# Fewer warming matmuls, a smaller first session, an earlier piece of w_out and re-placed sessions in a fused attention and feed-forward kernel

## The chip, the cores and the metric

One core of a Trainium2 chip. The metric is the device time of one execution in microseconds (us), the median of several runs. All profiled runs told here are of the state called fast (within 1.5% of the kernel's fastest). The span of a trace is some 2 us shorter than the time. Runs of one kernel scatter by about 1 us here (314.31 to 315.16 for the kernel before in the last series), with one at 316.2 in another series, so differences below that need many runs and are told with an interval. The series ran on different chips, with the kernel before timed beside the others each time; its median was 314.70 to 314.82 in all of them.

## The reference, cut to what matters

```python
# q, k, v: (8 batches, 8 heads, 576 positions, 64); w_in (512, 2048), w_out (2048, 512)
scores = scale * q @ k.T;  mask = |i - j| <= 32;  attn = softmax(scores where mask)
x = (attn @ v) with heads side by side              # 4608 tokens x 512
h = x @ w_in
g = h >= 1 ? h : h <= -1 ? 0 : (h + 1)**2 / 4
out = g @ w_out
```

Attention only looks 32 positions to each side, so nearly all of the work is the two products of the feed-forward part.

## The kernel before: the parts that matter

The feed-forward part goes in steps a = 0, 1, ... 151. Step a works on the token tile t = a // 8 (256 tokens) and the block f = a % 8 of 256 hidden units: eight matmuls ("hp", w_in times xT, the attention output laid out for them), then ScalarE ("rr") and VectorE ("mx", "gT") make g of it. The products with w_out ("op") follow some steps later; for the first two tiles they are cut into *pairs* of eight matmuls, and a pair's result (its accumulator) is added up over several steps. Matmuls write to PSUM, the memory behind TensorE; a *pool* hands out buffers of it, and who asks for a buffer waits until the last reader of its former content is done. All attention work is hung into these steps by `at(step, ...)`, where a half step such as 13.5 means behind the pairs of step 13: `tposes` transposes q or k of a batch on TensorE and copies it out of PSUM on ScalarE and VectorE, `scores` makes masked scores and their exponentials ("pt"), one call being a *session* (its first matmuls, "bias", lay the mask), `sums` multiplies with v and with ones and divides, which gives xT. Before step 0 stands the start: batch 0's first positions go through all of this with TensorE otherwise empty, and matmuls on zeros (`keep_warm`, "z") are meant to keep its clock up.

```python
ps_h = tile_pool("ps_h", bufs=2, PSUM)      # hp of most steps
ps_s, ps_n = ...                            # one tile of two banks each: transposes, scores, sums
ps_o = tile_pool("ps_o", bufs=2, PSUM)      # accumulators of op, made after the start
# ... cut ...
keep_warm(14, ps_h, "hp")
qn[0, 0] = cast(q32, "qb", 5)               # waits for the load of q
qq = [tpose(0, n, 0, ...) ...]; kk = [tpose(0, n, 1, ...) ...]
scores(0, (0, 1), (0, 2), (0, 2), None)
scores(0, (0, 2), (0, 1), (2, 3), None, ps_n)     # the small session
scores(0, (1, 2), (0, 2), (0, 2), None, ps_p)
keep_warm(5, ...); e0 = sums(0, 0, 0, 256); keep_warm(2, ...); e1 = sums(0, 1, 0, 256, ps_p)
keep_warm(8, ...); e0(); e1()
# ... cut ...
pairs = [(8, 0), (9, 1), (10, 2), (11, 3), (12, 4), (13, 5), ...]    # (step, pair)
two_on_act = (1, 2, 7, 8, 9, 10, 11, 12)          # steps that square on ScalarE
# ... cut: the main loop ...
for a in range(...):
    flush()                                       # multiplications that finish xT, on VectorE
    hp = (ps_o if a in (6, 7) else ps_h).tile(...)
    # eight matmuls into hp; rr on ScalarE; mx and gT on VectorE (or mx on ScalarE)
    flush(); run(a)                               # what at(a, ...) has put here
    for x in post: pair(x)                        # the pairs of this step
    run(a + 0.5)
```

## Time and profile before

| | before |
|---|---|
| median of its runs | 314.72 us |
| span of the profiled run | 313.0 us (its time 315.1) |
| TensorE idle from 15 to 30 us, from 30 to 70 us | 2.45 us, 1.70 us |

The prediction below shows the rows on which it rests. One place that it tells in words only is step 13, the first scores of batch 1. The rows are TensorE's timeline of the kernel before, with start, length, engine, source line, result and operands:

```profile
38.58 1.20 PE L187 MATMUL tp<-ident,kn 128*64 128x128 bf16 x36
39.71 1.05 PE L445 MATMUL op<-w_out,gT 128*128 128x256 bf16 x8
40.59 1.04 PE L489 MATMUL hp<-xT,w_in 128*128 128x256 bf16 x8
41.56 0.41 PE L206 MATMUL bb<-bias,ident 64*64 64x512 bf16 x4
41.80 0.66 PE L227 MATMUL bb<-qT,kT 64*64 64x128 bf16 x16
42.39 1.05 PE L445 MATMUL op<-w_out,gT 128*128 128x256 bf16 x8
43.58 0.41 PE L206 MATMUL bb<-bias,ident 64*64 64x512 bf16 x4
```

How to read it: matmuls are pipelined, so the length of a row (1.05) is longer than its pitch. Take starts instead: 39.71, 40.59, 41.56 are eight matmuls each, 0.87 apart, plus 0.1 when the kind changes. So up to 41.56 TensorE streams. The 16 score matmuls have 0.66 where others of the kind have 0.42: a short stop inside, for the second copy of kT. From the pair at 42.39 to the masks at 43.58 it is 1.19 instead of 0.97: a hole of 0.22 that the bracketed waits do not show, because the modelled end of the pair covers it.

### The profile page before, as it was taken

What the parts mean: (1) busy time and instruction counts of PE and PEld (TensorE: products, weight loads), DVE (VectorE), ACT (ScalarE), POOL (GpSimd) and SP (SyncE); (2) the same over time, 40 slices, a digit from 0 to 9 for tenths busy, and PEclk for the clock granted to TensorE, in tenths of its full rate; (3) what the DMA queues carried; (4) which work ended last, traced back from release to release, by engine and by line L of the source; (5) the groups of instructions that cost most, each with busy time, mean ns of one, the idle gap of its engine ahead of it and who ended that gap; (6) DMA issues with size and microseconds to landing.
All of it is one profiled execution on the core that took longest, in us unless ns stands there. A gap on an engine that the chain in (4) does not pass through costs nothing.

```text
span 313.0 us, 8615 instructions
## 1 busy us (share of the span) xinstructions
PE 304.1 (97%) x3711; PEld 207.9 (66%) x3711; DVE 243.7 (78%) x380; ACT 196.2 (63%) x324; POOL 72.3 (23%) x88
## 2 busy tenths in 40 slices
PE   8988999999999999999999999999999999999995
PEld 3566878776666666666666666666666666666652
DVE  3359558878888888888888888888888888878760
ACT  2788886866765766567666666566676666654431
POOL 8797354653051314040604000000000000000000
PEclk9999999999999999999999999999999999999999
DMA  9999999999999989896996792006501000100111
GB/s 151 183 186 198 175 207 186 179 160 163 165 176 139 111 175 159 74 110 133 166 109 69 76 154 69 34 36 112 109 36 36 37 34 36 37 36 34 48 55 67
DMA packets 124102, 34.54 MB, mean 110 GB/s; under 512 B 108192, under 2 KB 119712, under 8 KB 124064
## 3 DMA queue, kind: packets, MB, share of 16 engines
q0 software_dynamic: 94720, 18.06, 77.9%
q1 hardware_dynamic: 29200, 15.63, 21.4%
q8 instruction: 29, 0.48, 0.6%
q10 hardware_dynamic: 144, 0.29, 0.4%
q14 instruction: 9, 0.07, 0.1%
HBM read 36.70 MB, written 9.44 MB: 147 GB/s over the span
## 4 chain that ended last, share of the span: by engine, by line
PE 90%; ACT 4%; DVE 3%; issue 1%; ACTq 0%
PE hp L489 38%; PE op L429 36%; PE bb L293 6%; PE op L445 4%; PE bb L227 2%; PE z L336 2%; ACT pt L235 2%; PE tp L187 1%; DVE xT L305 1%; ACT rc L300 1%; ACT lr L299 1%; DVE kT L190 1%; DVE qT L190 1%; DVE mx L500 1%; ACT rr L493 0%
## 5 line engine op out<-in xcount | busy, mean ns | idle before, releaser
L489 PE MATMUL hp<-xT,w_in 128*128 128x256 bf16 x1152 | 149.3, 273 | 2.0 <-DVE xT L308 1.2
L493 ACT ACTIVATE rr<-hp 128x512 f32<-128x512 f32 x144 | 85.6, 595 | 87.1 <-PE hp L489 86.2
L489 PEld LDWEIGHTS <-w_in 128*128 128x128 bf16 x1152 | 112.0, 98 | 41.6 <-issue 2.6
L429 PE MATMUL op<-w_out,gT 128*128 128x512 bf16 x512 | 130.4, 380 | 0.0
L500 DVE TENSOR_TENSOR mx<-hp,rr 128x512 f32<-128x512 f32 x136 | 93.7, 689 | 33.2 <-ACT rr L493 31.3
L501 DVE SCALAR_TENSOR_TENSOR gT<-rr,mx 128x512 bf16<-128x512 f32 x136 | 94.1, 692 | 4.6
L429 PEld LDWEIGHTS <-gT 128*128 128x128 bf16 x512 | 47.5, 98 | 36.8
L235 ACT ACTIVATE pt<-bb 128x1024 bf16<-128x1024 f32 (+1 forms) x33 | 33.2, 1012 | 4.6 <-PE bb L227 3.1
L106 POOL DMA_DIRECT2D vn<-in_v_dram x32 | 27.3, 864 | 35.4 <-PE bb L227 32.3
L305 DVE TENSOR_TENSOR xT<-bb,rc 128x512 bf16<-128x512 f32 (+1 forms) x32 | 21.0, 657 | 11.0 <-ACT rc L300 10.3
L434 ACT COPY osb<-op 128x512 f32<-128x512 f32 x32 | 18.6, 583 | 11.6 <-PE op L429 11.1
L300 ACT ACTIVATE rc<-lr 128x512 f32<-128x512 f32 (+2 forms) x40 | 23.5, 587 | 1.3
L299 ACT ACTIVATE lr<-bb 128x512 f32<-128x512 f32 (+2 forms) x40 | 22.0, 550 | 0.8 <-PE bb L293 0.7
L98 POOL DMA_DIRECT2D qn<-in_q_dram x10 | 12.2, 1222 | 43.1 <-DMA qT<-qn 37.8
L293 PE MATMUL bb<-pt,ones 64*64 64x256 bf16 (+3 forms) x352 | 19.5, 255 | 1.5 <-DVE kT L190 0.8
L201 DVE TENSOR_TENSOR pt<-pt,mask 128x1024 bf16<-128x1024 bf16 (+1 forms) x33 | 20.2, 613 | 0.1
L293 PE MATMUL bb<-pt,vn 64*64 64x128 bf16 (+3 forms) x712 | 18.2, 204 | 0.0
L293 PEld LDWEIGHTS <-ones 64*64 64x64 bf16 x352 | 10.2, 105 | 9.9 <-issue 9.9
L293 PEld LDWEIGHTS <-vn 64*64 64x64 bf16 x712 | 16.7, 107 | 0.0
L445 PE MATMUL op<-w_out,gT 128*128 128x256 bf16 x128 | 16.5, 273 | 0.0
L98 POOL DMA_DIRECT2D kn<-in_k_dram x10 | 12.1, 1214 | 10.0 <-DMA kT<-kn 3.8
L227 PE MATMUL bb<-qT,kT 64*64 64x128 bf16 x520 | 13.2, 217 | 0.3 <-DVE kT L190 0.2
(56 smaller groups left out, 120.8 us busy)
## 6 DMA issues: line engine op xcount, KB each, us to landing
out_dram<-osb SPq DMA_DIRECT2D x36, 256.0 KB, 2.3
vn<-in_v_dram POOLq DMA_DIRECT2D x32, 144.0 KB, 8.9
qn<-in_q_dram POOLq DMA_DIRECT2D x10, 288.0 KB, 7.4
kn<-in_k_dram POOLq DMA_DIRECT2D x10, 288.0 KB, 8.0
w_out<-in_moe_w_out_dram POOLq DMA_DIRECT2D x4, 512.0 KB, 12.5
w_in<-in_moe_w_in_dram POOLq DMA_DIRECT2D x12, 128.0 KB, 6.4
qn<-in_q_dram POOLq DMA_DIRECT2D x2, 576.0 KB, 13.5
kn<-in_k_dram POOLq DMA_DIRECT2D x2, 576.0 KB, 14.7
```

Of the source, the lines that this page charges most:

```text
L98: nc.gpsimd.dma_start(out=x[:, :, h], in_=src[b, NY * h:NY * h + NY].rearrange("y s d -> (y s) d") .rearrange("(u p) d -> p u d", p=128))
L106: nc.gpsimd.dma_start(out=vn[b][64 * a:64 * a + 64, :, h], in_=v[b, y:y + 2].rearrange("y s d -> (y s) d") .rearrange("(c r) d -> r c d", ...
L235: A.activation(p, ps[:, :, :128 * n].rearrange(like, y=m), AF.Exp, scale=D ** -0.5)
L293: nc.tensor.matmul(bb[HD[h], a, o + c0:o + c1], ones[HD[a]] if c is None else vn[b][HD[a], c, h], p(a, h), start=n == 0, stop=True, skip_g ...
L299: A.activation(lr[:, :, :D0], bb[:, :, D0:2 * D0], AF.Ln)
L300: A.activation(rc[:, :, :D0], lr[:, :, :D0], AF.Exp, scale=-1.0)
L429: nc.tensor.matmul(o, gT[tt // 2][:, j, 128 * (tt % 2):128 * (tt % 2) + 128], w_out[:, j], start=not done, stop=len(done) == 2 * NF - 1, s ...
L445: nc.tensor.matmul(o[:, tt], gT[p][:, j, 128 * tt:128 * tt + 128], w_out[:, j, 256 * half:256 * half + 256], start=not done, stop=len(done ...
L489: nc.tensor.matmul(hp[:, j], w_in[:, kk, 256 * f + 128 * j:256 * f + 128 * j + 128], xT[:, kk, r0:r0 + TB], start=n == 0, stop=n == 3)
L493: A.activation(rr, hp, AF.Relu, scale=0.5, bias=0.5)
L500: V.tensor_max(mx, hp, rr)
L501: V.scalar_tensor_tensor(g, rr, 1.0, mx, op0=ALU.min, op1=ALU.mult)
```

## The change

It means to start earlier (fewer warming matmuls, less in the small session), to fill the wait of step 8 with pair 0 (whose piece of w_out is therefore cut out and loaded ahead of the last two pieces of w_in), to give two score sessions different buffers, to square step 2 on VectorE and not on ScalarE, and to put other work between batch 2's transposes and the next user of their buffers.

```diff
-        keep_warm(14, ps_h, "hp")
+        keep_warm(11, ps_h, "hp")
...
-        scores(0, (0, 2), (0, 1), (2, 3), None, ps_n)
+        scores(0, (0, 2), (0, 1), (2, 3), None, ps_n, 32)      # 32 queries instead of 128
...
-        keep_warm(5, ps_h, "hp")
+        keep_warm(4, ps_h, "hp")
...
-        keep_warm(8, ps_h, "hp")
+        keep_warm(7, ps_h, "hp")
...
-    put(w[:4] + [(load_half, ...) ...] + w[4:])
+    put(w[:4] + [(load_half, ...) ...] + w[4:12])
+    put([(load_w_out, 0, 0, 4)] + w[12:])
...
-    pairs = [(8, 0), (9, 1), (10, 2), (11, 3), (12, 4), (13, 5), ...]
-    two_on_act = (1, 2, 7, 8, 9, 10, 11, 12)
+    pairs = [(6, 0), (8, 1), (9, 2), (10, 3), (11, 4), (13, 5), ...]
+    two_on_act = (1, 7, 8, 9, 10, 11, 12)
...
     # seq[n]: (sums, scores) of batch 1 and up, in order
-    at(14, seq[0][0], (*seq[1][0], ps_s))
-    sums of seq[2..5] at 18, 20, 22, 27;  scores of seq[0..6] at 13, 13.5, 16, 18, 20, 25, 27
+    at(13, seq[0][1]); at(13.5, (*seq[1][1], ps_n)); at(14, (*seq[0][0], ps_s), seq[1][0])
+    sums of seq[2..5] at 18, 21, 24, 27;  scores of seq[2..6] at 16, 18, 21, 25, 27
-    transposes of batch 2 at 19.5, 21.5
+    transposes of batch 2 at 19.5, 22.5
```

(The scheduling lines at the end are written shorter than in the file.)

More of the change, by code (lines that the diff above doesn't have):

```diff
@@ L111, in load_w_in, with load_w_out @@
                             in_=moe_w_in.rearrange("(h y d) f -> h d y f", h=2, d=64)[h][:, :, c0:c1])
-    def load_w_out(c, n):
-        nc.gpsimd.dma_start(out=w_out[:, 8 * n:8 * n + 8, 256 * c:256 * c + 256],
-                            in_=moe_w_out.rearrange("(ko ki) f -> ki ko f", ki=128)[:, 8 * n:8 * n + 8,
-                                                                                    256 * c:256 * c + 256])
+    def load_w_out(c, k0, k1):
+        nc.gpsimd.dma_start(out=w_out[:, k0:k1, 256 * c:256 * c + 256],
+                            in_=moe_w_out.rearrange("(ko ki) f -> ki ko f", ki=128)[:, k0:k1, 256 * c:256 * c + 256])
     early = ctx.enter_context(tc.tile_pool(name="early", bufs=1))
@@ L149 @@
     w += [(load_w_in, c, c + 256, h) for c in range(1536, DFF, 256) for h in range(2)]
-    put(w[:4] + [(load_half, 1, t, h) for t in range(2) for h in range(2)] + w[4:])
+    put(w[:4] + [(load_half, 1, t, h) for t in range(2) for h in range(2)] + w[4:12])
+    put([(load_w_out, 0, 0, 4)] + w[12:])
     P.tensor_copy(band[HD[1], 0:128], band[HD[1], 64:192])
@@ L154 @@
                       band[:, :x].rearrange("p (n j) -> p n j", n=1).to_broadcast([128, n, x]))
-    put([(load_w_out, 0, n) for n in range(2)] + [(load_rows, 1, t) for t in range(2)])
-    put([(load_v, 1, n) for n in range(4)] + [(load_w_out, 1, n) for n in range(2)])
+    put([(load_w_out, 0, 4, 8), (load_w_out, 0, 8, 16)] + [(load_rows, 1, t) for t in range(2)])
+    put([(load_v, 1, n) for n in range(4)] + [(load_w_out, 1, 8 * n, 8 * n + 8) for n in range(2)])
     put([(load_rows, 2, t) for t in range(2)] + [(load_v, 2, n) for n in range(4)])
@@ L209, in add_mask, with scores @@
                                  start=True, stop=False, skip_group_check=True)
-    def scores(b, ys, pars, cs, eng, pool=ps_s):
+    def scores(b, ys, pars, cs, eng, pool=ps_s, w=128):
         if b not in pt:
@@ L218, in scores @@
             cols = (ys[1] - ys[0]) * (pars[1] - pars[0]) * (cs[1] - cs[0])
-            add_mask([ps[:, h] for h in range(2)], cols, 128)
+            add_mask([ps[:, h] for h in range(2)], cols, w)
         for y1 in range(*ys):
@@ L226, in scores @@
                             s0 = S * (y1 + 2 * a) + 64 * c
-                            nc.tensor.matmul(ps[HD[a], h, 128 * n:128 * n + 128], kT[b][HD[h], s0:s0 + 64],
-                                             qTs[b % 3][HD[h], PAD + s0 - 32:PAD + s0 + 96],
+                            nc.tensor.matmul(ps[HD[a], h, w * n:w * n + w], kT[b][HD[h], s0:s0 + 64],
+                                             qTs[b % 3][HD[h], PAD + s0 - 32:PAD + s0 - 32 + w],
                                              start=eng is not None, stop=True, skip_group_check=True)
                     n += 1
-        p = pt[b][:, :, ys[0]:ys[1], pars[0]:pars[1], 128 * cs[0]:128 * cs[1]]
+        p = pt[b][:, :, ys[0]:ys[1], pars[0]:pars[1], 128 * cs[0]:128 * cs[1] - 128 + w]
         m = 2 if n > cs[1] - cs[0] else 1
@@ L234, in scores @@
         like = "p h (y j) -> p h y j"
-        A.activation(p, ps[:, :, :128 * n].rearrange(like, y=m), AF.Exp, scale=D ** -0.5)
+        A.activation(p, ps[:, :, :w * n].rearrange(like, y=m), AF.Exp, scale=D ** -0.5)
         mask(eng, p, mask4[:, :256 * n].rearrange("p (h j) -> p h j", h=2).rearrange(like, y=m))
@@ L377 @@
     NF = DFF // 256
-    pairs = [(8, 0), (9, 1), (10, 2), (11, 3), (12, 4), (13, 5), (15, 6), (15, 8), (16, 7), (17, 9)]
-    two_on_act = (1, 2, 7, 8, 9, 10, 11, 12)
+    pairs = [(6, 0), (8, 1), (9, 2), (10, 3), (11, 4), (13, 5), (15, 6), (15, 8), (16, 7), (17, 9)]
+    two_on_act = (1, 7, 8, 9, 10, 11, 12)
     ev = {}
@@ L399 @@
     seq = [x for b in range(1, B) for x in steps(b, 224)]
-    at(14, seq[0][0], (*seq[1][0], ps_s))
-    for n, a in enumerate((18, 20, 22, 27)):
+    at(13, seq[0][1])
+    at(13.5, (*seq[1][1], ps_n))
+    at(14, (*seq[0][0], ps_s), seq[1][0])
+    at(16, seq[2][1])
+    for n, a in enumerate((18, 21, 24, 27)):
         at(a, seq[2 + n][0])
-    for n, a in enumerate((13, 13.5, 16, 18, 20, 25, 27)):
-        at(a, seq[n][1])
+    for n, a in enumerate((18, 21, 25, 27)):
+        at(a, seq[3 + n][1])
     sl = [30, 32, 35, 39, 42, 45, 49, 52, 56, 59, 62, 65, 69, 73, 77, 81, 84, 88, 92]
@@ L408 @@
         at(a, seq[6 + n][0], seq[7 + n][1] if n < len(sl) - 1 else None)
-    for b, *a in ((1, 11, 12), (2, 19.5, 21.5)):
+    for b, *a in ((1, 11, 12), (2, 19.5, 22.5)):
         for t in range(2):
```

## The prediction

> **What bounds the kernel now.** I read the page's busy table first, then the waits of TensorE in its timeline, then VectorE and ScalarE around each wait. In a timeline row the first number is the start, the second the length, both in us; the bracket is the idle time before it and what ended it.
>
> ```profile
> PE 304.1 (97%) x3711; PEld 207.9 (66%) x3711; DVE 243.7 (78%) x380; ACT 196.2 (63%) x324; POOL 72.3 (23%) x88
> ```
>
> TensorE is the bound; only its idle time and its useless work can be had. The table by stretches says where:
>
> ```profile
> 15.00:30.00 15.00, 12.55 (x243) 9.71 (x242) 10.80 (x18) 12.70 (x23) 12.71 (x18) 1.00 1.37 191
> 30.00:70.00 40.00, 38.30 (x614) 32.08 (x613) 28.91 (x44) 29.64 (x48) 19.89 (x21) 1.00 2.00 182
> 70.00:300.00 230.00, 230.00 (x2646) 154.95 (x2645) 196.22 (x298) 142.78 (x238) 27.40 (x28) 1.00 0.82 92
> ```
>
> From 70 us on TensorE is busy without a hole (230.00 of 230.00), so whatever it is ahead or behind at 70 us is carried to the end unchanged. The holes are 2.45 us before 30 us and 1.70 us from 30 to 70. TensorE's timeline names them:
>
> ```profile
> 1.19 6.11 PE L336 MATMUL z<-warm 128*128 128x512 bf16 x14 [1.19 <-DVE warm L127]
> 7.13 0.67 PE L189 MATMUL tp<-ident,qb 128*128 128x128 bf16 x9
> ...
> 18.75 1.03 PE L489 MATMUL hp<-xT,w_in 128*128 128x256 bf16 x8 [0.37 <-DMA w_in<-in_moe_w_in_dram]
> ...
> 23.42 1.03 PE L489 MATMUL hp<-xT,w_in 128*128 128x256 bf16 x8 [0.23 <-DMA w_in<-in_moe_w_in_dram]
> ...
> 29.40 1.03 PE L489 MATMUL hp<-xT,w_in 128*128 128x256 bf16 x8 [1.17 <-DVE xT L308]
> ...
> 59.98 0.30 PE L293 MATMUL bb<-pt,ones 64*64 64x256 bf16 x4 [0.76 <-DVE qT L190]
> ...
> 66.31 0.28 PE L293 MATMUL bb<-pt,ones 64*64 64x192 bf16 x4 [0.77 <-DVE kT L190]
> ```
>
> The matmuls of feed-forward step a ("hp", eight of 256 columns, pitch 0.87) stand at 18.75 for a=2, 23.42 for a=4, 29.40 for a=8. Two of these are anchored on w_in pieces that only the DMA stream can move; 29.40 is anchored on VectorE, which from 25.07 works in one unbroken row:
>
> ```profile
> 25.07 0.62 DVE L305 TENSOR_TENSOR xT<-bb,rc 128x448 bf16<-128x448 f32 x1 [0.55 <-ACT rc L300]
> 25.61 0.68 DVE L500 TENSOR_TENSOR mx<-hp,rr 128x512 f32<-128x512 f32 x1
> 26.33 0.69 DVE L501 SCALAR_TENSOR_TENSOR gT<-rr,mx 128x512 bf16<-128x512 f32 x1
> 26.94 0.62 DVE L305 TENSOR_TENSOR xT<-bb,rc 128x448 bf16<-128x448 f32 x1
> 27.47 0.68 DVE L500 TENSOR_TENSOR mx<-hp,rr 128x512 f32<-128x512 f32 x1
> 28.19 0.69 DVE L501 SCALAR_TENSOR_TENSOR gT<-rr,mx 128x512 bf16<-128x512 f32 x1
> 28.80 0.55 DVE L308 TENSOR_TENSOR xT<-bb,rc 128x384 bf16<-128x384 f32 x1
> 29.27 0.68 DVE L500 TENSOR_TENSOR mx<-hp,rr 128x512 f32<-128x512 f32 x1
> ```
>
> **What the Trainium skill says.** "TensorE: Matmul & The Clock Gate", Part 1, gives the array half clock until about one busy window of 3.4 us, 426.7 ns per 512-column matmul cold and 215.7 warm. The trace agrees in size: 14 warming matmuls fill 1.19 to 7.13, 0.42 each, and the nine transposes after them take 0.67, that is warm; so the clock came up near 7.1, 5.9 us after the first matmul. Part 4 of the page says that transposes do not count as busy in the same way; no row of the kernel before tests that. Part 2 says that matmuls stay in program order and only weight loads are pulled ahead: a waiting matmul holds up all behind it, as the 1.17 at 29.40 did.
>
> **The change part by part.**
>
> *Warming and the small session.* The queries land and are cast by 5.84 (VectorE's cast row, 5.05 + 0.79). With 14 warming matmuls the transposes start at 7.13; with 11 the stream ends at 1.19 + 11 x 0.427 = 5.89. The nine q transposes then run cold, 0.107 each (estimate, a quarter of a 512-column cold matmul), to 6.85; the k half issued second at 1.95 lands 4.9 us later, at 6.85, so its transposes start near 7.0. VectorE's two copies (pitch 0.63) end about 8.5 instead of 9.19, and scores start some 0.8 earlier. The small session's exponential goes from 512 to 128 elements a partition: ScalarE's pitch over the three sessions is 0.92 for 1024 and 0.48 for 512, so 0.86 ns an element, 384 fewer is 0.33. The two warming matmuls of 0.216 taken out later only fit the shorter wait. Sum: the first xT is ready about 1.1 us earlier, step 1 ends about 16.1 instead of 17.2.
>
> *What becomes of these 1.1 us.* The second halves of k are issued last at 10.99 and land 6.3 later, 17.28; w_in for a=2 at 12.27 plus 6.4, 18.6; w_in for a=4 at 16.37 plus 6.9, 23.3. The stream in front of them is the same bytes in the same order. So hp of a=2 stays at 18.75 and hp of a=4 at 23.42: TensorE just waits longer, about 1.5 before 18.75 and 1.1 before 23.42. Of this part I expect 0 at the end, and nearly 0 as well if the clock came up later.
>
> *ScalarE and VectorE to step 8.* They do gain: the q and k copies end 1.1 earlier, and a=2 no longer squares on ScalarE (0.63). I put the multiplication at 25.07 at 24.45. But next comes mx of a=4, which needs rr of a=4, which needs hp of a=4, anchored: rr from 24.50 instead of 24.95, mx from 25.11 instead of 25.61. From there the row above repeats unbroken, 0.50 earlier: xT at 28.30 to 28.85, mx of a=6 at 28.77 to 29.45.
>
> *Pair 0 at a=6.* Its eight matmuls (0.87) move ahead of the wait of 1.17; w_out's piece of 256 KB lands at about 25.04 + 1.3 = 26.4 (512 KB took 2.6 between landings), and the last w_in at 27.7, in time. With xT at 28.9, a gain of 1.3 would seem due. But the pair takes a buffer of the two-buffer PSUM pool that hp of a=6 and a=7 use as well. Pair 0's accumulator holds one over several steps, so hp of a=7 must take that of a=6, and wait until mx of a=6 has read it: 29.45, start 29.50. Before, at 29.40 TensorE had done hp of a=7 and not pair 0; now, at 29.50, pair 0 and not hp of a=7. Equal work: 0.10 later. Expected gain of the move: none.
>
> *Pair 4 from a=12 to a=11.* Before, pair 4 and hp of a=13 filled the 1.75 between the k transposes (38.58 to 39.71) and the scores. Now only hp does. The copies hang on rr of a=12, which moves with hp of a=12: 37.61 before, now 38.57 (0.10 behind plus pair 4 ahead of it, 0.87). So the second copy of kT ends at 42.00 + 0.96 = 42.96, and TensorE stands about 1.0 before or inside the scores: 0.95 behind.
>
> *Session of 13.5 to the other pool.* Before, its masks waited for the exponential of the session at 13: the pair of a=13 at 42.39, masks at 43.58, about 0.30 of hole. That goes: 0.62 behind.
>
> *Batch 2 and its sums.* The sums at a=20 and 22 sat right behind the transposes and waited for their copies in the same pool: 0.76 and 0.77 in the rows, 0.92 and 0.93 if counted from the last matmul's stream instead of its modelled end (start to start 1.82, less 0.87). At a=21 and 24 there are another hp and an output group of 0.87 each between; the copies end some 1.8 after the transposes, so both holes close: -1.85.
>
> Sum at 70 us: +0.10 + 0.85 - 0.33 - 1.85 = -1.23. Time 314.74 - 1.23 = 313.5; I predict **313.4**, since I may have made the stall of a=13 a little too long.
>
> **The rivals.** (1) The step-7 buffer does not bind (the pool finds another, or the mx comes sooner). For it: the author moved pair 0 there to fill the 1.17. Then steps 7 and 8 run on at 28.1 and 29.0, 1.3 more is gained, and the time is about 312.1. Against it: two buffers, and the accumulator is live. (2) The start is worth what it looks like, 1.1 us to the end: 312.4. Against it, the two DMA waits that are there already in the kernel before. (3) The clock comes up a whole window later because transposes do not count: scores run cold, the first xT comes near 15.5 as before, and the slack before 18.75 and 23.42 swallows it: the time stays about 313.5. If the clock stayed low beyond 23 us it would cost microseconds, 316; I give that 2%. (4) The stalls of a=20 and 22 move rather than go, to the scores of batch 2 at a=25: 314.5 to 315. The copies will have been done for two steps, so I doubt it.
>
> **Range and chances.** Main line 313.5, rival 1 at 312.1, rival 4 at 314.5: 8 times in 10 between 312.0 and 314.2. Two per cent is 6.3 us, more than all holes after the start together (4.15 in the table), so faster 0.01, within 0.98, slower 0.01.
>
> **What would show each step.** hp of a=2 still near 18.75 and of a=4 near 23.42 with longer DMA waits: anchors right. hp of a=7 waiting for VectorE's mx (L500) until about 29.5: buffer right; hp of a=8 waiting for xT or nothing: wrong. Scores near 43 behind the kT copies with a hole of about 1: right. No wait on copies near 60 and 66: right. VectorE's q-copy at start near 7.1 instead of 7.84: clock and casts right. I would be wrong altogether if the w_in pieces land more than half a microsecond apart from before, as all steps to a=8 hang on them.

## The result, and the profile after

The changed kernel took 313.94 us, median of 4 runs, against 314.72 for the kernel before: ratio 0.9977, 95% interval 0.996 to 0.9994. Measured again with 10 runs it took 313.95 against 314.78, ratio 0.9973, interval 0.9964 to 0.9983. By the 2% rule that is "same"; it is 0.85 us faster by the second ratio. A ratio is the mean time of one kernel's fast runs over that of the other's of the same rounds, so it is not quite the ratio of the medians quoted. Outputs were correct, here and in every experiment.

TensorE's timeline of the changed kernel, the places that answer to those of before:

```profile
1.19 4.87 PE L336 MATMUL z<-warm 128*128 128x512 bf16 x11 [1.19 <-DVE warm L126]
5.91 1.07 PE L189 MATMUL tp<-ident,qb 128*128 128x128 bf16 x9
...
18.04 1.03 PE L492 MATMUL hp<-xT,w_in 128*128 128x256 bf16 x8 [0.48 <-DMA w_in<-in_moe_w_in_dram]
...
22.13 1.05 PE L492 MATMUL hp<-xT,w_in 128*128 128x256 bf16 x8
...
26.07 1.04 PE L448 MATMUL op<-w_out,gT 128*128 128x256 bf16 x8
29.01 1.91 PE L492 MATMUL hp<-xT,w_in 128*128 128x256 bf16 x16 [1.91 <-DVE mx L503]
```

The transposes of q begin 1.22 us earlier, cold as expected. Step 2 still waits for its w_in. Step 4 (22.13) does not: here the prediction's second anchor was not there. Pair 0 runs at 26.07, and then TensorE stands for 1.91 us: steps 7 and 8 (16 matmuls in one row, pitch 0.87 each) begin at 29.01, released by VectorE's mx. VectorE's timeline of the changed kernel shows which mx:

```profile
27.81 0.55 DVE L308 TENSOR_TENSOR xT<-bb,rc 128x384 bf16<-128x384 f32 x1
28.28 0.68 DVE L503 TENSOR_TENSOR mx<-hp,rr 128x512 f32<-128x512 f32 x1
```

xT, for which step 8 waited before, is there at 28.36. The mx that follows it is that of step 6, and it ends at 28.96; step 7 starts 0.05 later. The wait for data has become a wait for a buffer.

Step 13 of the changed kernel, again TensorE's timeline:

```profile
39.07 1.20 PE L187 MATMUL tp<-ident,kn 128*64 128x128 bf16 x36
40.20 1.05 PE L492 MATMUL hp<-xT,w_in 128*128 128x256 bf16 x8
41.90 0.41 PE L206 MATMUL bb<-bias,ident 64*64 64x512 bf16 x4 [0.65 <-DVE kT L190]
42.11 0.24 PE L227 MATMUL bb<-qT,kT 64*64 64x128 bf16 x2
42.53 0.41 PE L227 MATMUL bb<-qT,kT 64*64 64x128 bf16 x14 [0.18 <-DVE kT L190]
42.88 1.05 PE L448 MATMUL op<-w_out,gT 128*128 128x256 bf16 x8
43.85 0.41 PE L206 MATMUL bb<-bias,ident 64*64 64x512 bf16 x4
```

Only hp lies between the transposes and the masks now. From hp to the masks it is 1.70 where 0.97 is free of waits, so 0.73 stand open by the starts (0.65 in the bracket), and about 0.38 more inside the scores, between the first two and the other 14. The masks of 13.5 follow their pair after 0.97: that little hole is closed. And around batch 2's transposes:

```profile
58.45 1.05 PE L492 MATMUL hp<-xT,w_in 128*128 128x256 bf16 x8
59.33 1.04 PE L448 MATMUL op<-w_out,gT 128*128 128x256 bf16 x8
60.20 1.04 PE L492 MATMUL hp<-xT,w_in 128*128 128x256 bf16 x8
61.17 0.30 PE L293 MATMUL bb<-pt,ones 64*64 64x256 bf16 x4
```

The sums come after two more groups and wait for nothing; the same holds at 68.41. The table by stretches of the changed kernel closes the account up to 70 us:

```profile
15.00:30.00 15.00, 12.33 (x242) 9.61 (x241) 12.19 (x18) 10.96 (x20) 13.89 (x19) 1.00 1.39 198
30.00:70.00 40.00, 39.01 (x619) 32.40 (x618) 29.09 (x45) 31.25 (x51) 19.68 (x20) 1.00 2.01 182
```

Idle 2.67 instead of 2.45 in the first stretch, 0.99 instead of 1.70 in the second. One warning on the page of this run: it shows TensorE busy for 297.6 us and 95%, and the group of 128x512 op matmuls as x477, although both kernels have 512 of them (the weight loads of the group are x512 here too). Records are missing, 35 x 0.215 = 7.5 us of stream. It is not idle time and no mark of the change: 12 of the 14 traces show x477, the second one of the kernel before among them, and the stretch from step 25 to the end takes 241.9 us in all 14. The short holes "released by issue" (0.32 by the starts) before op rows after 69 us are the places of the missing ones.

### The profile page after: what moved, and what is told of

Its sections match the earlier page's. It is cut to its first block, busy times and chain, and to the rows that moved or that the text cites. A ratio compares the mean times of both kernels' runs of the same rounds, so it can differ in the third digit from the quotient of the medians.

```text
span 311.6 us, 8569 instructions
## 1 busy us (share of the span) xinstructions
PE 297.6 (95%) x3669; PEld 207.2 (66%) x3706; DVE 244.9 (79%) x381; ACT 195.3 (63%) x323; POOL 73.5 (24%) x89
## 4 chain that ended last, share of the span: by engine, by line
PE 91%; DVE 3%; ACT 3%; issue 3%; ACTq 0%
PE hp L492 39%; PE op L432 35%; PE bb L293 6%; PE op L448 4%; PE bb L227 2%; PE z L336 2%; PE tp L187 1%; DVE kT L190 1%; DVE xT L305 1%; ACT rc L300 1%; DVE mx L503 1%; ACT rr L496 1%; ACT lr L299 1%; DVE gT L501 0%; ACT mx L500 0%
## 5 line engine op out<-in xcount | busy, mean ns | idle before, releaser
L432 PE MATMUL op<-w_out,gT 128*128 128x512 bf16 x477 | 123.0, 379 | 5.1 <-issue 4.9
L504 DVE SCALAR_TENSOR_TENSOR gT<-rr,mx 128x512 bf16<-128x512 f32 x137 | 95.3, 696 | 4.7
L227 PE MATMUL bb<-qT,kT 64*64 64x128 bf16 (+1 forms) x520 | 13.1, 217 | 0.4 <-DVE kT L190 0.4
```

Of the source, the lines that this page charges most:

```text
L432: nc.tensor.matmul(o, gT[tt // 2][:, j, 128 * (tt % 2):128 * (tt % 2) + 128], w_out[:, j], start=not done, stop=len(done) == 2 * NF - 1, s ...
L504: V.scalar_tensor_tensor(g, rr, 1.0, mx, op0=ALU.min, op1=ALU.mult)
```

## The experiments

All are single edits on the kernel before or on the changed one; each was timed in five rounds against the kernel before. First a table, then each in turn.

| kernel | median | ratio to before, 95% interval |
|---|---|---|
| before, again | 314.71 | 0.9997 (0.9989 to 1.0006) |
| before + start | 314.73 | 0.9997 (0.9989 to 1.0005) |
| before + pairs, w_out order, step 2 | 315.86 | 1.0041 (1.0029 to 1.0054) |
| before + pool of 13.5 | 314.49 | 0.9993 (0.9985 to 1.0001) |
| before + batch 2 | 312.99 | 0.9945 (0.9933 to 0.9957) |
| changed, again | 313.95 | 0.9973 (0.9964 to 0.9983) |
| changed, old start | 314.22 | 0.9981 (0.9974 to 0.9989) |
| changed, pair 4 at step 12 | 313.52 | 0.9956 (0.9939 to 0.9973) |
| changed, step 7 in ps_h | 312.97 | 0.9936 (0.9920 to 0.9952) |
| changed, both of these | 312.68 | 0.9928 (0.9909 to 0.9947) |
| changed, step 6 in ps_h | 312.36 | 0.9923 (0.9910 to 0.9937) |
| changed, step 6 in ps_h, pair 5 at step 12 | 311.61 | 0.9905 (0.9891 to 0.9918) |

### The kernel before, again

No edit.

> The kernel before, unchanged, for its run-to-run spread. Open: in the changed kernel's trace the w_in piece for step 4 was in by 22.1 us, in the kernel before's at 23.4. Theory A (the DMA stream's arrival varies from run to run): this trace has hp of step 4 somewhere between 22.1 and 23.4 us, and hp of step 8 between 28.4 and 29.4. Theory B (the change moved the arrival): hp of step 4 at 23.4 within 0.2, hp of step 8 at 29.4 within 0.2. Time 314.7 in both, ratio 1.000 within 0.001.

Its trace has steps 4 and 8, in TensorE's timeline, at

```profile
22.83 1.03 PE L489 MATMUL hp<-xT,w_in 128*128 128x256 bf16 x8
...
29.02 1.03 PE L489 MATMUL hp<-xT,w_in 128*128 128x256 bf16 x8 [0.96 <-DVE xT L308]
```

that is 0.59 and 0.38 earlier than in the first trace of the same kernel. Theory A holds: the arrival of w_in varies from run to run. Here the piece landed at 22.69 and in the first trace at 23.28. The version with batch 2 alone, whose program is the same up to step 19, had step 4 at 22.40. Over the traces of this study the second w_in piece of step 4 landed between 21.84 and 23.52. The trace that the prediction read was a late one, and its time, 315.1, above the median. The traces show two shares: GpSimd issued the piece between 15.40 and 16.37, after waits that differ from trace to trace, and from issue to landing it took 6.3 to 7.5. Why these vary is open; nothing here tests it.

### The start alone

```diff
 # on the kernel before
-        keep_warm(14, ...) ... keep_warm(5, ...) ... keep_warm(8, ...)
+        keep_warm(11, ...) ... keep_warm(4, ...) ... keep_warm(7, ...)
-        scores(0, (0, 2), (0, 1), (2, 3), None, ps_n)
+        scores(0, (0, 2), (0, 1), (2, 3), None, ps_n, 32)
```

> The kernel before with the start alone changed: 11 warming matmuls, the others 4 and 7, the small session of 32 queries. Theory (what the start gains is swallowed by the waits for w_in at steps 2 and 4): first xT about 1 us earlier, hp of step 8 within 0.3 us of 29.2, time 314.6, ratio 0.999 to 1.0. Rival (the gain is kept, since in most runs w_in is there by 22 us): 313.8, ratio 0.997.

Ratio 0.9997: nothing gained, as the theory has it. In its trace TensorE restarts step 0 with the full xT at 14.47 (15.57 and 15.12 in the two traces of before), but these two are late ones: the other four traces with the old start have 14.75 to 14.90, all eight with the new one 14.47 to 14.83. On the mean the start brings 0.35 us to step 0, not one. Then step 2 stands at 18.28 (18.75, 18.54 before), and step 8 at 28.77, a little outside the 0.3 that I had allowed, behind VectorE's xT; counted from step 2 it is 10.49, as in the second trace of before (10.48). In this trace the bracket at step 2 names VectorE's gT, but w_in's piece landed at 18.14, and 0.14 from landing to start is what the rows that name the load have too (18.62 to 18.75 in the kernel before). It is the load that step 2 waits for; the name in a bracket is that of the release which the profile puts last.

### The pairs, the order of w_out and step 2 alone

```diff
 # on the kernel before
+ put([(load_w_out, 0, 0, 4)] + w[12:])
+ pairs = [(6, 0), (8, 1), (9, 2), (10, 3), (11, 4), (13, 5), ...]
+ two_on_act = (1, 7, 8, 9, 10, 11, 12)
```

> The kernel before with only w_out's first piece ahead of the last of w_in, the pairs earlier (0 at step 6, 1 to 4 one step earlier) and step 2 squared on VectorE. Theory (step 7 waits for the buffer of step 6, and pair 4 is missing behind the kT copies): nothing at step 8 within 0.3, and 0.85 lost at step 13: 315.4, ratio 1.002 to 1.003. Rival (pair 0 fills the wait for xT): 313.9.

1.29 us slower (0.0041 x 314.7), more than the 0.85 expected; the rival is out. TensorE's timeline of this version:

```profile
29.24 1.91 PE L489 MATMUL hp<-xT,w_in 128*128 128x256 bf16 x16 [1.35 <-DVE mx L500]
...
42.11 0.41 PE L206 MATMUL bb<-bias,ident 64*64 64x512 bf16 x4 [0.64 <-DVE kT L190]
```

The same two holes as in the changed kernel. From step 7's start to the pair behind step 13's first scores it is 43.09 - 29.24 = 13.85 (42.88 - 29.01 = 13.87 in the changed kernel), from step 8's start in the kernel before 42.39 - 29.40 = 12.99, with as many matmuls between: 0.86 to 0.88 lost at step 13, as predicted. The rest, 0.4, is not between step 13 and the end, where the starts keep their distances, so it must lie ahead of step 7. Its start is 0.22 after step 8's in the second trace of before and 0.16 ahead of that in the first, so a single pair of traces, taken so, does not settle this term. Counted from step 2, which waits for its w_in in every trace, they agree: step 7 comes 10.88 to 10.97 after it in the five traces that have this wait on mx, step 8 10.48 to 10.65 in the five with pair 0 at step 8. The means differ by 0.36.

### The pool of 13.5 alone

```diff
 # on the kernel before
- at(14, seq[0][0], (*seq[1][0], ps_s))         # scores of 13 and 13.5 both in ps_s
+ at(13, seq[0][1]); at(13.5, (*seq[1][1], ps_n)); at(14, (*seq[0][0], ps_s), seq[1][0])
```

> The kernel before with only the session of 13.5 moved to the other pool (and the two sums of step 14 with their pools exchanged). Theory: the masks of 13.5 no longer wait 0.30 for the exponential of 13, hp of step 14 comes 0.3 earlier after step 13: 314.4, ratio 0.999. Rival (the sums of step 14 then wait for the exponential instead): 314.7, ratio 1.000.

Ratio 0.9993, the interval just touching 1: 0.22 us by the mean, the sign of the theory but not clear of noise. The starts in the traces agree with 0.2: pair of 13 to hp of 14 takes 1.76 before and 1.54 in this version and in the changed kernel. The rival is out by this version's trace: from hp of 14 to hp of 15, over the sums, it is 1.83, and 1.82 before.

### Batch 2 alone

```diff
 # on the kernel before
- sums at 18, 20, 22, 27; scores8 at 20; transposes of batch 2 at 19.5, 21.5
+ sums at 18, 21, 24, 27; scores8 at 21; transposes of batch 2 at 19.5, 22.5
```

> The kernel before with only the sums of batch 1 at steps 21 and 24 instead of 20 and 22, and batch 2's second transposes at 22.5. Theory: both holes behind the copies go (0.93 each from the stream), nothing takes their place: 312.85, ratio 0.994. Rival (they move to a later step): 313.8 or more.

312.99, a gain of 0.0055 x 314.7 = 1.73 us: the theory, nearly to the digit. From hp of step 14 to hp of step 25 the traces have 26.95 before and 25.28 here, 1.67 less, and 25.28 in the changed kernel. Nothing took the place of the two holes. This part alone is faster than the whole change.

### The changed kernel, again, and with the old start

> The changed kernel, unchanged, since its first measurement had only 4 runs and an interval of 0.996 to 0.9994. The parts measured alone add up: start -0.1, pairs +1.3, batch 2 -1.7, pool of 13.5 -0.2, together -0.7 us, ratio 0.9977; if the true ratio lies below 0.996, the parts help each other, above 0.999 they hinder each other. Step 7 behind mx near 29.0, step 13's second half near 42.5, whatever the arrival of w_in for step 4.

Ratio 0.9973. The parts alone sum to -0.09 + 1.29 - 0.22 - 1.73 = -0.75 us; the whole is -0.85 here. The parts neither help nor hinder each other beyond noise. Step 7 stood behind mx until 29.23, and the last 14 of step 13's scores at 42.74.

> The changed kernel with the old start (14, 5 and 8 warming matmuls, small session of 128 queries). Theory (the start gives nothing to the end): 313.9, as the changed kernel. Rival (it gives some of its 1.1 us where w_in is in early): 314.3 or more.

Ratio 0.9981 against 0.9973: 0.25 us by the means, and the intervals overlap, so it is not told from nothing. In its trace step 7 starts at 29.17, between the 29.01 and 29.23 of the two traces of the changed kernel.

### Step 7 out of the shared pool

```diff
 # on the changed kernel
-            if a in (6, 7):          # hp of steps 6 and 7 from ps_o
+            if a == 6:
```

> The changed kernel with hp of step 7 in the pool of the other steps, so that it need not wait for the buffer of hp of step 6. Theory (the buffer is what stops step 7): step 7 starts near 27.0 us without a wait, step 8 waits for xT alone and starts near 28.4 instead of 29.9, the 1.5 us are kept to the end: 312.5. Rival (the buffer hides another wait, of a late w_in piece or of VectorE's row, that ends at the same time): step 7 or 8 still starts near 29 and the time stays at 313.9.

312.97: the wait on mx was the buffer's, and about 1 us came back, not 1.5. The trace says where the rest went (TensorE's timeline):

```profile
27.58 1.91 PE L492 MATMUL hp<-xT,w_in 128*128 128x256 bf16 x16
...
30.69 1.03 PE L492 MATMUL hp<-xT,w_in 128*128 128x256 bf16 x8 [0.33 <-DVE gT L501]
```

Steps 7 and 8 run without a wait, although in this run w_in of step 4 came late (0.80 of wait at 22.93). But now steps 7, 8 and 9 share the two buffers of ps_h, and step 9 waits until gT of step 7 has read its hp: 0.49 by the starts, which is what is missing.

### Pair 4 back at step 12

```diff
 # on the changed kernel
-    pairs = [..., (11, 4), (13, 5), ...]
+    pairs = [..., (12, 4), (13, 5), ...]
```

> The changed kernel with pair 4 back at step 12. Theory (moved to step 11 it no longer fills the time of the kT copies): the hole of 0.8 before the masks of step 13 goes, scores end 0.87 us earlier, 313.1. Rival (the hole is made by VectorE's queue and comes whatever TensorE does): the second half of the scores still at 42.5, 313.9.

313.52: half of the 0.87 expected by the medians (0.43), a third by the starts (step 7 to step 14 takes 15.12 instead of 15.41). The hole at step 13 goes, but one step earlier TensorE's timeline has

```profile
38.90 1.34 PE L187 MATMUL tp<-ident,kn 128*64 128x128 bf16 x36 [0.64 <-DVE qT L190]
```

The transposes of k use the buffers of those of q, and with pair 4 gone from step 11 they come before q's copies are out. There are two places to fill, behind q and behind k, and one pair to fill them. Neither theory nor rival had that: the hole was moved, and only the part that did not fit was won.

### Both

> Both of the two edits on the changed kernel. Theory: they add up, 1.5 + 0.9 less than 313.9, that is 311.6. Rival (one of them only moves the wait to the next transfer or buffer): not below 312.4.

312.68 median, runs from 312.0 to 313.4. That is not the sum of what was expected of the two edits (311.6), but within the noise the sum of what each had given alone: 313.95 - 0.98 - 0.43 = 312.54. Its trace holds the two new waits of its parents (step 9, k's transposes), and in it w_in of step 4 was the latest of all traces, with step 8 at 29.18 (28.45 in the version with step 7 moved):

```profile
23.65 1.03 PE L492 MATMUL hp<-xT,w_in 128*128 128x256 bf16 x8 [1.29 <-DMA w_in<-in_moe_w_in_dram]
```

That such lateness makes the wide spread of its times is a guess; one trace of this kernel doesn't show it.

### Step 6 out of the shared pool

```diff
 # on the changed kernel
-            if a in (6, 7):
+            if a == 7:
```

> The changed kernel with only hp of step 6 in the other steps' pool, pair 5 where it was. Theory (the buffer of step 6 is the whole of what pair 0 lost): step 7 and pair 0 run on, step 8 starts when xT is there, near 28.5 with xT in VectorE's row at 27.9 to 28.5 and not 29.9; 1.4 less than the changed kernel, 312.5, and unlike the version with step 7 moved no wait of step 9 on gT. Rival: like the version with step 7 moved, 313.0.

312.36, the 312.5 expected, and the buffer is the whole of what step 7 waited for: step 7 has ps_o's free buffer, and step 9 finds that of step 6, whose mx is long done. TensorE's timeline:

```profile
27.34 1.04 PE L492 MATMUL hp<-xT,w_in 128*128 128x256 bf16 x8
28.65 1.03 PE L492 MATMUL hp<-xT,w_in 128*128 128x256 bf16 x8 [0.27 <-DVE xT L308]
```

Step 8 starts 28.65 instead of 29.88 (29.01 + 0.87), when xT is there.

### The best version: that, and pair 5 at step 12

```diff
 # on the changed kernel
-    pairs = [..., (11, 4), (13, 5), ...];  if a in (6, 7)
+    pairs = [..., (11, 4), (12, 5), ...];  if a == 7
```

> The changed kernel with hp of step 6 instead of step 7 in the pool of the other steps (so that hp of 7 and pair 0 have a buffer each and hp of 9 finds one free), and pair 5 at step 12 instead of 13, behind the kT copies, pair 4 staying at 11. Theory: no wait of step 7 on mx, none of step 9 on gT, hole at step 13 down from 1.15 to about 0.3, with up to 0.3 new at the sums of step 14: 311.9. Rival (the time is then set by w_in's arrival, which varies by over 1 us): between 312.0 and 313.0 with a spread of 1 us from run to run.

311.61, ratio 0.9905: 3.0 us less than the kernel before and 2.3 less than the changed one. Pair 4 fills the place behind q, pair 5 the place behind k. In TensorE's timeline hp of step 13 begins at 39.70, and the scores of both sessions follow it, with a stop of 0.1 inside the first (0.44 to the next start, where 16 such matmuls take 0.33 to 0.36 without one):

```profile
40.91 0.65 PE L227 MATMUL bb<-qT,kT 64*64 64x128 bf16 x16
41.35 0.43 PE L206 MATMUL bb<-bias,ident 64*64 64x512 bf16 x4
```

The expected new stop at the sums of step 14 came too, 0.29 by the starts.

## Why the prediction was right, and where it was off

The time on record, 313.4 with 312.0 to 314.2, holds the measured 313.94. The predicted gain was 1.23 by its sum, the measured 0.72 and 0.85.

Counted from start to start, the traces split the whole account into stretches that hardly scatter. "Pair 0 early" are the kernel after (two traces), pairs alone, old start and pair 4 at step 12; "pair 0 late" are the kernel before (two traces), the start alone, batch 2 alone and the pool of 13.5 alone.

| stretch, us | pair 0 late | pair 0 early |
|---|---|---|
| hp of step 2 to hp of step 8 (late) or 7 (early), as many matmuls ahead | 10.48 to 10.65, mean 10.55 | 10.88 to 10.97, mean 10.91 |
| from there to hp of step 14, old pool for 13.5 | 14.74, 14.75 | 15.61 |
| the same, new pool for 13.5, pair 4 at step 11 where pair 0 is early | 14.53 | 15.39 to 15.41 |
| hp of step 14 to hp of step 25, batch 2 as before; changed | 26.95; 25.28 | 26.96; 25.28 |
| hp of step 25 to the end | 241.9 | 241.9 |

1. **Warming and small session: right for the trace it was worked from.** The transposes started at 5.91 against 5.89 foretold, ran cold at 0.11 each, and VectorE's first copy moved to 7.02 against 7.1. What I had not seen is that 7.13, the start before, was the latest of many: six traces with 14 warming matmuls have the first transpose at 7.13, 6.68, 6.33, 6.31, 6.09 and 6.08, since the clock came up at different times (a 512-column matmul takes 0.42 cold and 0.216 warm, so 14 of them end later when it comes up late). With 11 it is 5.90 to 5.96 in all eight traces, as the cast of q ends near 5.85; in four of them the clock was up before. So the 1.1 foretold for the first xT is 0.35 on the mean at step 0. The Trainium skill, "TensorE: Matmul & The Clock Gate", Part 1, says that the window is free-running and the cold count varies from run to run; I cited the half clock from it and read over this.
2. **What becomes of it: result right, one of two reasons wrong.** Expected 0 at the end, measured 0.09 alone. Step 2 waited in every trace and began at 18.02 to 18.75; in three traces the bracket names VectorE's gT, but w_in landed 0.13 to 0.14 before the start in all 14. The anchor at step 4, "hp of a=4 at 23.42", failed: the w_in piece came at 21.84 to 23.52, and in seven of 14 traces step 4 follows the sums without a wait, in four more with one under 0.2. It was not needed: step 2 to step 8 takes 10.65 in the first trace, with a wait at step 4, and 10.63 in that of the pool of 13.5, with none. I named pieces that land more than half a microsecond off as what would make me wrong altogether. They did, and it did not: the kernel before scatters with them as well (step 8 at 28.73 to 29.40), so both sides of the difference move alike. That was luck, as the prediction had not thought of it.
3. **Pair 0: right in what it waits for, mis-sized by 0.26.** The buffer of step 6 holds step 7, on mx, in all five traces of the four versions that have pair 0 at step 6 and steps 6 and 7 in ps_o, at 29.00 to 29.24; taken away, 1.6 us came back (313.95 to 312.36). But the move costs 0.36 (10.91 less 10.55) where 0.10 was foretold. mx of step 6 ends 0.60 after the xT ahead of it, as foretold. The row that both stand in was to start 0.50 earlier, with the start and step 2's square as the reasons. From step 2 to its first multiplication it takes 6.22 on the mean with pair 0 late and 5.98 with it early, so it starts 0.24 earlier. The start has no share in that: 6.16 with it alone, 6.16 in the second trace of before.
4. **Pair 4: right,** 0.87 lost (15.61 less 14.74) against 0.85.
5. **Pool of 13.5: mis-sized.** 0.33 in the sum (0.30 in the text); the starts show 0.21 and the times 0.22. I had counted the change of kind between pair and masks (0.1) as part of the hole.
6. **Batch 2: mis-sized for the same reason.** 1.85 expected, 1.73 measured. The 0.93 from the stream contains 0.1 that every change from hp to sums takes; by the starts (59.98 to 58.17 is 1.81, with a free one taking 0.97) it is 0.84 and 0.85, together 1.69, and 1.67 over the whole stretch.
7. **Sum.** By the starts +0.36 + 0.87 - 0.21 - 1.67 = -0.65, where -1.23 was foretold and the times give -0.72 and -0.85, with 0.3 to each side for the second. Nearly all of the difference is in points 3, 5 and 6. Step 2 itself began at 18.43 on the mean with pair 0 late and at 18.22 with it early; five traces each, which scatter by 0.3 to 0.65, do not tell that from chance. The part with pairs, w_out and step 2 alone is 0.36 + 0.87 = 1.23 by the starts and 1.29 by the times. The 0.1 that the prediction took off its 313.5 for a stall of step 13 that might be shorter went the wrong way: that stall was right.

Of the rivals, 1 (the buffer does not bind) and 4 (the stalls of batch 2 move) were false; 2 (the start is worth 1.1) was false alone and in the whole; 3 (the clock comes up a window later) was in none of the traces.

## What to carry to other kernels

When work is moved into a wait, ask which buffer it takes and who else takes one from that pool before it is given back: here 0.87 us of filler put step 7 behind another step's last reader, and one word in the choice of pool was worth more than the change. When filler is moved from one place, look at the place that it leaves. And before a wait on a load is taken for an anchor, look at a second trace of the same kernel: this one moved by 0.6 us there and by 1.7 over all traces. Differences of a few tenths came out only when they were counted from the last event that such a load sets, here the start of step 2.

## What the Trainium skill lacked or had wrong

- "TensorE: Matmul & The Clock Gate", Part 4, says that the full clock does not engage for transposes, as they do not count as busy in the same way. The transposes of q did run at two rates here, 0.067 us each in the kernel before (7.13 to 7.73 for nine) and 0.11 in the changed one, so the full clock serves them. In four traces with 11 warming matmuls the clock came up while only transposes ran, by 7.04 us at the latest; as the warming matmuls had gone before, this does not show that transposes count.
- No page that I read says how far the landing of the same load varies between runs of the same program. Here one w_in piece landed at 23.28 and 22.69 in two traces of the same kernel, and between 21.84 and 23.52 us over 14 traces whose loads ahead of it are the same.
- "Perfetto Trace Analysis", Identifying Performance Opportunities, says that the same gap repeating for a stretch can mean too little SBUF or PSUM for the next tile. The buffer waits here come once each (1.91 us at step 7, 0.33 at step 9 in the version with step 7 moved), so a single gap can be one too.
- No page that I read says that a profile can lose the records of matmuls and keep those of their weight loads: 477 of 512 in one group in 12 of 14 traces. Two traces of the changed kernel, with and without the loss, show TensorE busy for 297.6 and 302.3 us, with spans of 311.6 and 311.8.
